# A Nyström attention and gated feed-forward kernel with the next pair's turns and sums, the Z product and the attention pieces placed elsewhere

## The chip, the cores and the metric

The kernel runs on one core of one Trainium2 chip. The metric is the device time of one execution in microseconds. Three runs of the kernel before took 339.7, 344.31 and 350.49 us (median 344.31). In the text PE is TensorE, DVE is VectorE, ACT is ScalarE, POOL is GpSimd, and SP is SyncE, which here only issues DMAs.

## The reference

Batch 8, 8 heads, 576 rows, head dimension 64. Queries and keys are averaged over groups of 18 rows to 32 landmarks; three softmaxes follow, a 32 by 32 matrix is inverted by six steps, and the product goes through a gated feed-forward.

```python
q_lm = q.reshape(B, H, m, S // m, D).mean(axis=3)          # m = 32
k_lm = k.reshape(B, H, m, S // m, D).mean(axis=3)
A  = sm(q, k_lm);  Bm = sm(q_lm, k_lm);  C = sm(q_lm, k)   # softmax of scale * a @ b.T
Z  = Bm.T / (norm1(Bm) * norminf(Bm) + 1e-6)               # per head
for _ in range(6):
    Z = 2 * Z - Z @ Bm @ Z
x = A @ Z @ C @ v                                          # heads side by side: 4608 x 512
out = ((x @ w1) * (x @ w2)) @ w3 @ w_out
```

## The kernel before, in words

The kernel folds the last two weight matrices into one, `w34 = w3 @ w_out`, and it never forms the attention output: C v and Z give a small matrix per head, which is multiplied into w1 and w2 ("G"), so that "U" computes both feed-forward inputs straight from the normalised A. All order is written by hand: the scheduler is off, and two strings of tokens, `PROLOGUE` and `PERIOD`, say in which order the pieces are issued to the five in-order engine queues. Batches go in pairs: while pair p is in its U and D work, the attention pieces of pair p+1 run between, and pair p+2 is loaded. There are four pairs and so four runs of `PERIOD`, called periods 0 to 3 here; the last has only U and D work.

The tokens, with two digits for batch of the pair and head half: F, one of 32 folding slots (two `prod` matmuls, and in every second slot a turn of a piece of w3); K, a load of q or k with cast (POOL queue); T, its transposing DMA (SP queue); L, its sums to landmarks on POOL (on DVE in `Y`, for pair 0); X, the exchange of the two half sums and the landmark matrices `lmk` and `qbd`; C, scores of the landmarks against k with exp on ACT and partial sums `es` on POOL; V, their product with v (`W` loads v); A, scores of q; B, SM, R, I0 to I5, the landmark matrix and its inversion; S, denominators of A; N, normalised A (`ahat`); Z, the small matrix `zt`; G, `gproj`; U, `up_unit` (8 matmuls, a cast on ACT, a product `ab` on DVE); D, `down_chunk` (8 matmuls, a copy on ACT, two stores); w, a load of w1 or w2 (POOL queue); E, the copy of a head's w1 and w2 to the other 64 partitions. A mark ' means the pair after. PSUM has 8 banks: `big` takes two and `small` one. In the prologue there is one `big` buffer, in the periods three.

Of the kernel before, what the change touches and what calls it, by code (L numbers as in the profile page):

```python
# [46 lines left out]
def kernel(  # L47
# [101 lines left out]
    def sums(b, t, eng):  # L149
        lp = pz.tile([128, H, 32], FP32, name="lp", bufs=4)  # L150
        tt = sts[b][t + "T"]
        if eng is nc.vector:
            nc.vector.tensor_reduce(out=lp, in_=tt.rearrange("p h j (l g) -> p h l j g", g=3),
                                    axis=AX.XY, op=ALU.add)
        else:
            s = pz.tile([128, H, P], FP32, name="ls", bufs=1)
# [1 line left out]
            eng.tensor_tensor(out=s, in0=s, in1=tt[:, :, 2, :], op=ALU.add)
            s3 = s.rearrange("p h (l g) -> p h l g", g=3)
            eng.tensor_tensor(out=lp, in0=s3[:, :, :, 0], in1=s3[:, :, :, 1], op=ALU.add)  # L160
            eng.tensor_tensor(out=lp, in0=lp, in1=s3[:, :, :, 2], op=ALU.add)
# [74 lines left out]
    def istep(p, it):  # L236
# [15 lines left out]
        else:  # L252
# [3 lines left out]
            tbd = pz.tile([128, 4, 4, 32], FP32, name="tbd", bufs=1)  # L256
            for x in range(2):
                nc.vector.tensor_tensor(
                    out=tbd[:, 2 * x:2 * x + 2],
                    in0=t6[:, 2 * x:2 * x + 2].unsqueeze(2).to_broadcast([128, 2, 4, 32]),  # L260
# [367 lines left out]
```

## Time and profile before

| | before |
|---|---|
| three runs | 339.7, 344.31, 350.49 us |
| profiled execution | 342.35 us, of which span 340.6 us |
| PE busy | 286.8 us, 84% |
| PE weight load | 164.0 us, 48% |
| DVE busy | 171.8 us, 50% |
| ACT busy | 123.8 us, 36% |
| POOL busy | 116.5 us, 34% |
| DMA | 46.68 MB, mean 137 GB/s |

Busy shares are averages over stages with different limits. The chain that ended last runs mostly through PE (19% of the span, more than all the other engines together), and the PE row of the 40 slices has its only 0 in the slice from 42.6 to 51.1 us.

### The profile page before, as it was taken

The numbers are of one execution on the slowest core, as the hardware profiler recorded it, in microseconds if no ns is written. First come the engines' busy times: TensorE is split into PE (matmuls) and PEld (weight loads), VectorE is DVE, ScalarE is ACT, GpSimd is POOL, SyncE is SP. The second block draws the span as 40 slices with busy tenths as digits, with TensorE's granted clock in tenths as the row PEclk, the third lists the DMA queues.
The fourth block names the chain that finished last, engine by engine and source line by source line (L and its number), as shares of the span: only waits on it lengthen the run. The fifth ranks groups of instructions, "written<-read, shape, count | busy, mean of one in ns | idle before, by whom it ended". The sixth has DMA issues, their size and how long they took to land. (4 is left out here: it accounts for less than half of the span.)

```text
span 340.6 us, 8360 instructions
## 1 busy us (share of the span) xinstructions
PE 286.8 (84%) x3584; PEld 164.0 (48%) x3584; DVE 171.8 (50%) x313; ACT 123.8 (36%) x209; POOL 116.5 (34%) x138
## 2 busy tenths in 40 slices
PE   3795705999978986687999998598999899999994
PEld 2243304655533355554545665353566664456651
DVE  6026340533895232658665357957426676624320
ACT  2013101421222344232565643245564435534532
POOL 2001401500399626309597430848762000000000
PEclk9998765999979998989999999879999999999998
DMA  8999998399999400497999289899932021132234
GB/s 203 295 258 175 174 219 188 53 210 185 176 226 213 89 2 2 65 172 122 194 213 230 64 125 167 126 183 203 231 81 49 28 60 36 31 93 64 69 84 126
DMA packets 66437, 46.68 MB, mean 137 GB/s; under 512 B 39264, under 2 KB 57696, under 8 KB 66400
## 3 DMA queue, kind: packets, MB, share of 16 engines
q1 hardware_dynamic: 49408, 28.32, 41.5%
q0 software_dynamic: 13600, 11.54, 23.6%
q10 hardware_dynamic: 3392, 6.29, 5.8%
q8 instruction: 28, 0.46, 0.6%
q14 instruction: 9, 0.07, 0.1%
HBM read 38.80 MB, written 9.44 MB: 142 GB/s over the span
## 5 line engine op out<-in xcount | busy, mean ns | idle before, releaser
L402 DVE TENSOR_TENSOR ab<-a_sb,big 128x576 f16<-128x576 f16 x64 | 48.2, 752 | 68.0 <-ACT a_sb L401 60.4
L395 PE MATMUL big<-ahat,gt 128*128 128x288 f16 x512 | 78.0, 296 | 4.1 <-DVE gt L380 1.9
L473 PE MATMUL psw<-wof,w3t 128*128 128x512 f32 x128 | 67.7, 659 | 1.8 <-DMA wof<-in_moe_w_out_dram 1.8
L423 PE MATMUL small<-w,ab 128*128 128x512 f16 x288 | 67.5, 380 | 0.3
L395 PEld LDWEIGHTS <-gt 128*128 128x128 f16 x512 | 48.2, 101 | 28.6 <-issue 11.1
L401 ACT CAST a_sb<-big 128x576 f16<-128x576 f32 x64 | 40.7, 636 | 25.1 <-PE big L395 22.7
L423 PEld LDWEIGHTS <-ab 128*128 128x128 f16 x288 | 26.8, 98 | 30.7 <-issue 2.5
L425 ACT ACTIVATE o_sb<-small 128x512 f32<-128x512 f32 x36 | 21.5, 597 | 53.1 <-PE small L423 53.1
L473 PEld LDWEIGHTS psw<-wof,w3t 128*128 128x128 f32 x128 | 23.9, 206 | 26.7 <-issue 23.2
L281 POOL TENSOR_TENSOR e<-ect 96x384 f32<-96x384 f32 x16 | 16.0, 998 | 52.3 <-ACT ect L276 49.8
L86 POOL DMA_DIRECT2D nat<-in_k_dram x8 | 6.4, 799 | 69.7 <-DMA kT<-nat 69.5
L292 PE MATMUL small<-vt,ect 96*32 96x64 f32 x768 | 15.0, 229 | 14.1 <-DMA vt<-in_v_dram 13.8
L380 DVE TENSOR_SCALAR gt<-big 128x1024 f16<-128x1024 f32 x16 | 19.2, 1216 | 8.6 <-PE big L373 8.6
L292 PEld LDWEIGHTS small<-vt,ect 96*32 96x32 f32 x768 | 12.2, 115 | 18.5 <-DMA vt<-in_v_dram 14.7
L373 PE MATMUL big<-wdup,zt 128*32 128x512 f16 x256 | 19.6, 384 | 1.4 <-DVE gt L380 0.9
L466 DVE COPY w3t<-pst 128x512 f32<-128x512 f32 x8 | 5.5, 692 | 28.5 <-PE pst L461 28.4
L378 ACT ACTIVATE gt<-big 128x1024 f16<-128x1024 f32 x16 | 16.4, 1023 | 7.5 <-PE big L373 7.4
L244 PE MATMUL small<-sz 32*32 32x64 f32 (+1 forms) x768 | 15.2, 217 | 4.3 <-DVE sz L250 2.7
L271 PE MATMUL big<-qbd,kT 128*96 128x64 f16 x192 | 12.6, 222 | 6.5 <-POOL qbd L176 3.0
L476 ACT CAST w<-psw 128x512 f16<-128x512 f32 x8 | 4.7, 585 | 34.7 <-PE psw L473 24.1
L276 ACT ACTIVATE ect<-big 96x768 f32<-96x768 f32 x16 | 12.8, 806 | 10.3 <-PE big L271 10.3
L244 PEld LDWEIGHTS small<-sz 32*32 32x32 f32 x768 | 11.5, 107 | 10.4 <-DVE sz L250 3.3
(85 smaller groups left out, 316.0 us busy)
## 6 DMA issues: line engine op xcount, KB each, us to landing
vt<-in_v_dram SPq DMA_DIRECT2D x8, 1152.0 KB, 12.3
nat<-in_k_dram POOLq DMA_DIRECT2D x8, 576.0 KB, 6.4
nat<-in_q_dram POOLq DMA_DIRECT2D x8, 576.0 KB, 9.2
out_dram<-o_sb SPq DMA_DIRECT2D x24, 192.0 KB, 2.3
w3f<-in_moe_w_dram ACTq DMA_DIRECT2D x16, 256.0 KB, 6.6
out_dram<-o_sb SPq DMA_DIRECT2D x24, 128.0 KB, 2.4
wof<-in_moe_w_out_dram ACTq DMA_DIRECT2D x4, 512.0 KB, 9.9
wdup<-in_moe_w_dram POOLq DMA_DIRECT2D x2, 1024.0 KB, 15.0
```

Source lines behind the costliest of these rows:

```text
L244: nc.tensor.matmul(psI[sl, 64 * a:64 * a + n], src[sl, a, 32:64], src[sl, a, 0:n], start=True, stop=True, tile_position=(32 * h, 32 * h))
L281: nc.gpsimd.tensor_tensor(out=e3, in0=ect[:, 0:3], in1=ect[:, 3:6], op=ALU.add)
L292: nc.tensor.matmul(psV[32 * h:32 * h + 32, 0:64], st["ect", qd][:, c, h, :], st["v"][:, 4 * qd + h, c, :], start=(c == 0), stop=(c == TK - 1),
L373: nc.tensor.matmul(psG[32 * h:32 * h + 32, n, :], st["zt"][:, 4 * qd + h, :], wdup[:, 4 * qd + h, w, 512 * n:512 * n + 512], start=True, s ...
L378: nc.scalar.activation(out=dst, in_=psG, func=AXF.Copy, scale=1.0 / ZS)
L380: nc.vector.tensor_scalar(out=dst, in0=psG, scalar1=1.0 / ZS, scalar2=None, op0=ALU.mult)
L395: nc.tensor.matmul(p[:, c, 0:HS], st["g", qd][:, w, 128 * j:128 * j + 128], st["ahat", qd][:, c, :], start=(qd == 0), stop=(qd == 1))
L401: nc.scalar.copy(out=a_sb, in_=p[:, :, 0:HS])
L402: nc.vector.tensor_tensor(out=ring["ab"][:, j, off:off + S].rearrange("p (c s) -> p c s", c=2), in0=a_sb, in1=pp[1][:, :, 0:HS], op=ALU.mult)
L423: nc.tensor.matmul(pso[:, :], w, w34[:, j, :], start=(j == 0), stop=(j == 7))
L425: nc.scalar.activation(out=o_sb, in_=pso[:, :], func=AXF.Copy, scale=1.0 / (X64 * X64))
L473: nc.tensor.matmul(psw[j], w3ts[j, c // 4][:, c % 4, :], wof[:, c, :], start=(c == 0), stop=(c == 7))
```

## The change

The strings are rewritten. The prologue has no N for batch 1 of pair 0 and two of its G pieces no more; these follow in the first period, marked +, which means "of the pair whose U work runs". A third string, `FIRST`, is used for period 0, and `PERIOD` for the others; the mark " loads three pairs ahead. Turns and sums (T and L) of the pair after the next begin in the first half of a period. `zmat` is done once for a pair, by 16 matmuls on 32 by 32 tiles of `t6`, where two masked block-diagonal products were; the mask and `tbd` are gone. The denominators stay in PSUM for reciprocal, cast and mix. The sums on POOL are cut in two halves of four heads each. The copies of the folding turns and of the exchange run on ACT.

```diff
+PROLOGUE = """
+F F F F F F F F F Y0 F F F Y1 F C00 F C01 w0 F A00 F A01 w1 F F B F SM C10 'Kk0 'Kq0 F R V00 F V01 I0 'Tk0 F C11 I1 'Kk1 F A10 I2 'Tq0 F V10 I3 'Lk0 'Kq1 E0 E1 F V11 A11 I4 F S0 I5 'Tk1 'Lq0 E2
+F E3 E4 E5 F N00 Z E6 E7 F N01 'Tq1 'W0 'W1 F G000 S1 'Lk1 F G001 F G010 'Lq1 F G011
+"""
+FIRST = """
+U +G100 'Kk0 'Kq0 U +G110 X0 U +G101 +N10 C00 U +N11 +G111 C01 X1 U A00 V00 'Tk0 U A01 V01 B 'Kk1 U SM C10 'Tq0 U A10 C11 'Kq1
+U R 'Lk0 D I0 V10 U I1 A11 'Lq0 D I2 V11 'Tk1 U I3 'Tq1 D I4 S0 U I5 'Lk1 D N00 S1 'W0 U Z N01 'W1 'Lq1 U G000 'X0 "Kk0 U G001 "Kq0 U G010 G011
+"""
 PERIOD = """
-U C00 D C01 U X1 A00 D V00 U A01 C10 D V01 B U C11 SM D V10 'Kk0 U R A10 D I0 V11 'Kq0 U I1 'Tk0 U S0 I2 'Tq0 'Kk1 U A11 I3
-U N00 'Lk0 I4 'Tk1 'Kq1 D N01 S1 U I5 'Lq0 'Tq1 D Z0 'W0 'W1 U N10 Z1 U N11 G000 D 'Lk1 G010 U 'X0 G001 U G011 D G100 'Lq1 U G110 U G101 G111
+U +G100 C00 D +G110 C01 U X1 +G101 'Tk0 A00 D V00 A01 'Kk1 +N10 U +G111 'Tq0 D B 'Kq1 V01 'Lk0 U SM C10 D A10 C11 'Lq0 U R D +N11 I0 U I1 A11 'Tk1 U V10 I2 U V11 I3 'Tq1 'Lk1
+U I4 D I5 S0 'X0 U Z 'Lq1 'W0 D N00 S1 'W1 U N01 G000 "Kk0 D G001 "Kq0 U G010 D G011 U U U U
 """
...
-PROLOGUE = """
-F F F F F F F Y0 F F C00 C01 F A00 Y1 F w0 V00 C10 F V01 C11 B F SM 'Kk0 A01 F 'Kq0 V10 R F I0 A10 'Tk0 F I1 S0 w1 F I2 V11 'Tq0 'Kk1 F N00 I3 'Tk1 'Kq1 F N01 I4 A11 'Lk0 F I5 'Tq1
-S1 F 'Lq0 E0 Z0 E1 F E2 E3 N10 Z1 F E4 E5 N11 F E6 E7 G000 'Lk1 F G010 'W0 F 'X0 G001 'W1 F G011 'Lq1 F G100 F G110 F G101 F G111 F
-"""
...
-            s = pz.tile([128, H, P], FP32, name="ls", bufs=1)
-            eng.tensor_tensor(out=s, in0=tt[:, :, 0, :], in1=tt[:, :, 1, :], op=ALU.add)
...
+            for h0 in range(0, H, 4):
+                hs = slice(h0, h0 + 4)
+                s = pz.tile([128, 4, P], FP32, name="ls", bufs=1)
+                eng.tensor_tensor(out=s, in0=tt[:, hs, 0, :], in1=tt[:, hs, 1, :], op=ALU.add)
...
-            nc.vector.tensor_copy(out=lx[t][0:64], in_=st["lp" + t][64:128])
+            (nc.scalar.copy if eng is nc.gpsimd else nc.vector.tensor_copy)(
+                out=lx[t][0:64], in_=st["lp" + t][64:128])
...
-        ect = pat.tile([P, TK, 4, 32], FP32, name="ect", bufs=2)
+        ect = pat.tile([P, TK, 4, 32], FP32, name="ect", bufs=3)
...
-        rr = pz.tile([128, QS], FP32, name="rr", bufs=1)
-        nc.vector.reciprocal(out=rr, in_=psS[:, 0:QS])
+        rr = psS[:, 0:QS]
+        nc.vector.reciprocal(out=rr, in_=rr)
...
+    def zmat(p):
+        t6 = prs[p]["t6"]
+        psZ = big()
+        for a in range(4):
+            xd = sts[2 * p + a // 2]["xd", a % 2]
+            for h in range(4):
+                sl = slice(32 * h, 32 * h + 32)
+                e = 64 * (h % 2)
+                nc.tensor.matmul(psZ[e:e + 64, h // 2, 32 * a:32 * a + 32], xd[sl, :], t6[sl, a, :],
+                                 start=True, stop=True, tile_position=(32 * h, e))
+        zt = pat.tile([128, 4, 2, 2, 32], FP16, name="zt", bufs=2)
+        for e in range(2):
+            pv_ = psZ[64 * e:64 * e + 64, :, 0:128].rearrange("p c (a m) -> p a c m", m=32)
+            nc.scalar.copy(out=zt[0:64, :, :, e, :], in_=pv_)
+            nc.vector.tensor_tensor(out=zt[64:128, :, :, e, :], in0=pv_, in1=zt[0:64, :, :, e, :],
+                                    op=ALU.subtract)
...
-        if cc == 0:
-            nc.vector.tensor_copy(out=dst, in_=pst)
-        else:
-            nc.scalar.copy(out=dst, in_=pst)
+        nc.scalar.copy(out=dst, in_=pst)
...
-        for tok in PERIOD.split():
+        for tok in (PERIOD if p else FIRST).split():
...
+            elif tok[0] == '"':
+                attn(p + 3, tok[1:])
+            elif tok[0] == "+":
+                attn(p, tok[1:])
```

Three places show what the tables move, all on POOL.

The first is POOL's queue in the middle of the prologue, before, from the fourth head half of C on (`e` and `es` are its partial sums, `nat` the loads of q and k of pair 1, `wdup` the load of w1 or w2, `ls` and `lp` the sums):

```order
L281 TENSOR_TENSOR e3_448<-ect_446 96x384
L283 TENSOR_TENSOR es_450<-e3_448 96x128
L284 TENSOR_TENSOR es_450<-es_450,e3_448 96x128
L86 DMA nat_495<-in_k_dram 96x8x384
L86 DMA nat_519<-in_q_dram 96x8x384
L489 DMA wdup_93<-in_moe_w2_dram 64x8x1024
L86 DMA nat_707<-in_k_dram 96x8x384
L86 DMA nat_747<-in_q_dram 96x8x384
L157 TENSOR_TENSOR ls_788<-kT_603 128x768
```

and of the change, from the second head half of C on:

```order
L283 TENSOR_TENSOR es_340<-es_340,e3_338 96x128
L486 DMA wdup_92<-in_moe_w1_dram 64x8x1024
L486 DMA wdup_92<-in_moe_w2_dram 64x8x1024
L280 TENSOR_TENSOR e3_451<-ect_449 96x384
L282 TENSOR_TENSOR es_453<-e3_451 96x128
L283 TENSOR_TENSOR es_453<-es_453,e3_451 96x128
L90 DMA nat_456<-in_k_dram 96x8x384
L90 DMA nat_458<-in_q_dram 96x8x384
L280 TENSOR_TENSOR e3_605<-ect_603 96x384
L282 TENSOR_TENSOR es_607<-e3_605 96x128
L283 TENSOR_TENSOR es_607<-es_607,e3_605 96x128
L90 DMA nat_628<-in_k_dram 96x8x384
```

Before, w1 goes out after the second half (not shown) and w2 behind the first two loads of pair 1; now both stand together, ahead of the first loads of pair 1.

The second is POOL's queue where pair 1's landmark matrices are made, before, at the end of the prologue (`lmk` and `qbd0` are X0):

```order
L160 TENSOR_TENSOR lp_921<-ls_922 128x256
L161 TENSOR_TENSOR lp_921<-lp_921,ls_922 128x256
L172 TENSOR_TENSOR lmk_958<-lp_787,lx_952 128x256
L176 TENSOR_TENSOR qbd0_89<-lp_847,lx_955 64x8x32 x2
L157 TENSOR_TENSOR ls_987<-qT_827 128x768
L158 TENSOR_TENSOR ls_987<-ls_987,qT_827 128x768
L160 TENSOR_TENSOR lp_986<-ls_987 128x256
L161 TENSOR_TENSOR lp_986<-lp_986,ls_987 128x256
L281 TENSOR_TENSOR e3_1091<-ect_1089 96x384
```

and of the change, in the first units of period 0:

```order
L161 TENSOR_TENSOR ls_992<-ls_992,qT_916 128x384
L163 TENSOR_TENSOR lp_986<-ls_992 128x128
L165 TENSOR_TENSOR lp_986<-lp_986,ls_992 128x128
L90 DMA nat_1040<-in_k_dram 96x8x384
L90 DMA nat_1042<-in_q_dram 96x8x384
L177 TENSOR_TENSOR lmk_1074<-lp_724,lx_1068 128x256
L181 TENSOR_TENSOR qbd0_88<-lp_848,lx_1071 64x8x32 x2
L280 TENSOR_TENSOR e3_1123<-ect_1121 96x384
```

X0 stood ahead of the last sum of pair 1; it now stands behind all four sums of that pair and behind two loads of pair 2.

The third is POOL's queue in period 1, before, between X1 and the third head half of C:

```order
L172 TENSOR_TENSOR lmk_2051<-lp_1806,lx_2045 128x256
L176 TENSOR_TENSOR qbd1_90<-lp_1903,lx_2048 64x8x32 x2
L281 TENSOR_TENSOR e3_2151<-ect_2149 96x384
L283 TENSOR_TENSOR es_2153<-e3_2151 96x128
L284 TENSOR_TENSOR es_2153<-es_2153,e3_2151 96x128
```

and of the change:

```order
L181 TENSOR_TENSOR qbd1_89<-lp_1852,lx_2062 64x8x32 x2
L90 DMA nat_2149<-in_k_dram 96x8x384
L90 DMA nat_2215<-in_q_dram 96x8x384
L160 TENSOR_TENSOR ls_2251<-kT_2079 128x384
L161 TENSOR_TENSOR ls_2251<-ls_2251,kT_2079 128x384
L163 TENSOR_TENSOR lp_2250<-ls_2251 128x128
L165 TENSOR_TENSOR lp_2250<-lp_2250,ls_2251 128x128
L160 TENSOR_TENSOR ls_2256<-kT_2079 128x384
L161 TENSOR_TENSOR ls_2256<-ls_2256,kT_2079 128x384
L163 TENSOR_TENSOR lp_2250<-ls_2256 128x128
L165 TENSOR_TENSOR lp_2250<-lp_2250,ls_2256 128x128
L280 TENSOR_TENSOR e3_2309<-ect_2307 96x384
```

Two loads and the whole first sum of pair 3 now stand ahead of the partial sums that V10 of pair 2 needs.

## Rows read from the trace of the kernel before

**Rows 1.** Windows by stage: start:end, length, busy per engine, PEclk, DMA share, GB/s.
```profile
0.00:122.90 122.90, 93.70 (x840) 47.44 (x841) 55.01 (x108) 24.45 (x42) 38.89 (x47) 0.90 0.97 184
122.90:179.50 56.60, 46.41 (x809) 29.66 (x809) 33.93 (x60) 25.31 (x43) 32.54 (x37) 0.94 0.73 119
179.50:240.90 61.40, 54.67 (x849) 32.53 (x849) 38.46 (x70) 28.66 (x48) 33.75 (x38) 0.94 0.88 159
240.90:295.20 54.30, 51.74 (x849) 31.06 (x850) 30.29 (x60) 27.82 (x46) 11.29 (x18) 1.00 0.28 70
295.20:327.20 32.00, 31.47 (x200) 19.51 (x200) 13.21 (x17) 14.24 (x25) 0.00 (x0) 1.00 0.27 69
327.20:340.60 13.40, 8.83 (x42) 3.83 (x40) 0.94 (x2) 3.37 (x6) 0.00 (x0) 0.92 0.43 112
```

**Rows 2.** Timeline of PE in the prologue: start, us, operation [idle before <- releaser].
```profile
19.14 3.60 PE L473 MATMUL psw<-wof,w3t 128*128 128x512 f32 x8
23.01 3.60 PE L473 MATMUL psw<-wof,w3t 128*128 128x512 f32 x8
...
34.25 3.76 PE L473 MATMUL psw<-wof,w3t 128*128 128x512 f32 x4
...
54.52 1.51 PE L292 MATMUL small<-vt,ect 96*32 96x64 f32 x48 [13.84 <-DMA vt<-in_v_dram]
```

**Rows 3.** Timeline of the waits in periods 0 and 1.
```profile
131.91 0.68 PE L271 MATMUL big<-qbd,kT 128*96 128x64 f16 x12 [2.70 <-POOL qbd L176]
...
214.60 1.65 POOL L157 TENSOR_TENSOR ls<-kT 128x768 f32<-128x768 f16 x1
...
214.75 1.60 DVE L333 CAST rhi<-rr 128x144 f16<-128x144 f32 x1
...
219.95 1.19 PE L355 MATMUL small<-tbd,xd 128*128 128x128 f32 x4 [3.30 <-DVE tbd L258]
```

**Rows 4.** Timeline of several engines, 37 to 51 us.
```profile
37.49 0.70 POOL L489 DMA_DIRECT2D wdup<-in_moe_w_dram  x1
...
47.37 2.55 DVE L153 TENSOR_REDUCE lp<-qT 128x256 f32<-128x2304 f16 x1 [4.53 <-DMA qT<-nat]
...
50.01 0.40 ACT L170 COPY lx<-lp 64x256 f32<-64x256 f32 x1 [6.67 <-DVE lp L153]
```

**Rows 5.** Landing times, by tile: weight halves, loads of q and k, turns of k.
```profile
DMA to landing us min/median/max: 13.5/15.0/16.4
...
DMA to landing us min/median/max: 5.0/7.1/18.1
...
DMA to landing us min/median/max: 5.8/8.4/16.9
```

**Rows 6.** Timeline of POOL, the first and last row of pair 1's sums.
```profile
88.62 0.77 POOL L86 DMA_DIRECT2D nat<-in_k_dram  x1 [21.60 <-DMA kT<-nat]
...
115.99 0.80 POOL L161 TENSOR_TENSOR lp<-lp,ls 128x256 f32<-128x256 f32 x1
```

**Rows 7.** Groups by line and form, POOL: busy, mean ns of one, idle before.
```profile
L281 POOL TENSOR_TENSOR e<-ect 96x384 f32<-96x384 f32 x16 | 16.0, 998 | 52.3 <-ACT ect L276 49.8 <-PE small L187 1.8 <-PE big L395 0.5
...
L157 POOL TENSOR_TENSOR ls<-kT 128x768 f32<-128x768 f16 x6 | 9.9, 1643 | 8.5 <-DMA kT<-nat 8.4
```

**Rows 8.** Timeline of PE in periods 1 to 3, for the pitch of the pieces.
```profile
198.37 0.45 PE L230 MATMUL small<-btn,bt 32*32 32x32 f32 x32 [0.21 <-DVE btn L220]
...
279.99 0.66 PE L355 MATMUL small<-tbd,xd 128*128 128x128 f32 x4
...
281.59 0.41 PE L343 MATMUL big<-rmix,selc 128*128 128x144 f16 x4
281.93 0.62 PE L373 MATMUL big<-wdup,zt 128*32 128x512 f16 x8
...
316.17 1.89 PE L423 MATMUL small<-w,ab 128*128 128x512 f16 x8
317.90 2.12 PE L395 MATMUL big<-ahat,gt 128*128 128x288 f16 x16
```

More of the change, by code (lines that the diff above doesn't have):

```diff
@@ L116, in constants @@
                                 base=0, pattern=[[-1, 128]], channel_multiplier=1)
-        nc.vector.memset(ones1, 1.0)
+        nc.vector.memset(ones1, 1.0 / ZS)
         for t in qbds:
@@ L155, in sums @@
         else:
-            s = pz.tile([128, H, P], FP32, name="ls", bufs=1)
-            eng.tensor_tensor(out=s, in0=tt[:, :, 0, :], in1=tt[:, :, 1, :], op=ALU.add)
[L158 to L161, printed above, removed]
+            for h0 in range(0, H, 4):
+                hs = slice(h0, h0 + 4)
+                s = pz.tile([128, 4, P], FP32, name="ls", bufs=1)
+                eng.tensor_tensor(out=s, in0=tt[:, hs, 0, :], in1=tt[:, hs, 1, :], op=ALU.add)
+                eng.tensor_tensor(out=s, in0=s, in1=tt[:, hs, 2, :], op=ALU.add)
+                s3 = s.rearrange("p h (l g) -> p h l g", g=3)
+                eng.tensor_tensor(out=lp[:, hs], in0=s3[:, :, :, 0], in1=s3[:, :, :, 1],
+                                  op=ALU.add)
+                eng.tensor_tensor(out=lp[:, hs], in0=lp[:, hs], in1=s3[:, :, :, 2], op=ALU.add)
         sts[b]["lp" + t] = lp
@@ L255, in istep @@
                                     op=ALU.add)
[L256 to L260, printed above, removed]
-                    in1=mask4.unsqueeze(1).to_broadcast([128, 2, 4, 32]), op=ALU.mult)
-            prs[p]["tbd"] = tbd
+            prs[p]["t6"] = t6
     def cscores(b, qd):
@@ L300, in cv @@
         nc.vector.reciprocal(out=rcr, in_=psV[:, 64:65])
-        xd = pz.tile([128, 2, 64], FP32, name="xd", bufs=4)
-        nc.scalar.activation(out=xd, in_=psV[:, 0:64].unsqueeze(1).to_broadcast([128, 2, 64]),
-                             func=AXF.Copy, scale=rcr[:, 0:1])
+        xd = pz.tile([128, 64], FP32, name="xd", bufs=4)
+        nc.scalar.activation(out=xd, in_=psV[:, 0:64], func=AXF.Copy, scale=rcr[:, 0:1])
         st["xd", qd] = xd
@@ L347, in norm_a @@
         st["ahat", qd] = a
-    def zmat(b):
-        st = sts[b]
-        x = b % 2
-        tbd = prs[b // 2]["tbd"]
-        psZ = small()
-        for qd in range(2):
-            nc.tensor.matmul(psZ[:, 128 * qd:128 * qd + 128],
-                             st["xd", qd].rearrange("p a d -> p (a d)"),
-                             tbd[:, 2 * x + qd].rearrange("p h m -> p (h m)"),
-                             start=True, stop=True)
-        zt = pat.tile([128, 8, 32], FP16, name="zt")
-        pzv = psZ[:, 0:256].rearrange("p (h m) -> p h m", m=32)
-        nc.scalar.activation(out=zt, in_=pzv, func=AXF.Copy, scale=ZS)
-        nc.vector.scalar_tensor_tensor(out=zt[64:128], in0=pzv[64:128], scalar=ZS,
-                                       in1=zt[64:128], op0=ALU.mult, op1=ALU.subtract)
-        st["zt"] = zt
+    def zmat(p):
[14 more added lines that the diff above has]
+                                    op=ALU.subtract)
+        for x in range(2):
+            sts[2 * p + x]["zt"] = zt[:, 2 * x:2 * x + 2].rearrange("p a c e m -> p (a c e) m")
     def gproj(b, qd, w):
@@ L503, in attn @@
             return bnorm(p)
+        if tok == "Z":
+            return zmat(p)
         if kind in "BR":
@@ L516, in attn @@
             return exchange(b, nc.gpsimd)
-        if kind == "Z":
-            return zmat(b)
         if kind == "S":
```

5 lines of the change are left out of this document (1 added, 4 removed).

## The prediction

> **What bounds the kernel now.** I read the trace by stage first, because the busy shares of the page average over stages with different limits. The windows [rows 1] give the prologue 122.9 us, periods 0 to 3 56.6, 61.4, 54.3 and 32.0 us, and the tail 13.4 us. PE is the longest engine in each. In period 3 it is full: 31.5 of 32.0 us. Period 2 is the yardstick of a whole period: 9 D, 16 U and all attention pieces in 54.3 us at granted clock 1.00, with POOL at 11.3 us, since no sums are left there. Period 1 holds the same pieces and needs 7 us more, and period 0, which runs 5 D fewer (D has a pitch of 1.73 us [rows 8]), needs 2.3 us more where it should need 8.7 us less. So some 11 us of period 0 and 7 us of period 1 are waits, and much more of the prologue: PE is busy in 93.7 of 122.9 us.
>
> The timeline says which waits. In the prologue PE stands for 13.8 us before the first V, until v has landed [rows 2], and the fold slot after an idle stretch takes 3.76 us where a warm pair of slots takes 3.60 us [rows 2]; that is the lower clock, worth about 2 us each time. In period 0, C waits 2.70 us for the landmark matrix that POOL makes, and in period 1, Z waits 3.30 us for the masked product on DVE; that product was late because a cast of DVE took 1.60 us, from 214.75 on, beside a 1.65 us sum of POOL that began at 214.60 [rows 3].
>
> **The change, part by part.** I add up the new time from five stretches, against the span of 340.6 us of the profiled execution.
>
> *The prologue up to the first C of period 0.* V is asked for only after 20 fold slots, so the wait for v goes. What is late next: ACT's exchange copies for the second batch wait for DVE's sum of q, which waited 4.53 us for its turn and began at 47.37 [rows 4]; ACT also carries the exps, so the second C of the new order, with one `big` buffer, stops PE until then. A weight load went out at 37.49 [rows 4] beside that turn, and in the new order it is not yet out. So the sum of q begins between 42.8 (no wait) and 47.4; I take 44, nearer the first. With 2.55 us for the sum and 0.40 us for the copy, PE goes on at about 48, having stood about 9 us after 14 fold slots.
>
> From there a chain on POOL and the DMAs decides. Two rounds of C, exp and partial sums (estimate 6 us, from 1.0 us for `e` alone [rows 7]) put both weight loads out at about 53. They stand together ahead of pair 1's loads on one queue. One lands after 13.5 to 16.4 us [rows 5]: both may be through after 16.4 us if they share nothing else (69), or after twice 16.4 (86); I take twice 13.5, so 80, because the 15 us of one were measured beside other traffic that is there still. The load of k follows at its shortest, 5.0 us, as it has waited in line, and its turn at its shortest, 5.8 us, as the weights that slowed it are through [rows 5]: 91. Then the old chain from the landing of that turn, 88.62, to the last sum, 116.8, took 28.2 us [rows 6]; four sums, one X and two loads lay in it. The new one has two loads more at 0.77 us each, and does not wait for the q turn between. A sum is now eight halves: half of 1643 ns is 0.82 us, and the 384-element row `e` costs 998 ns [rows 7], so a sum is between as long as before and 1 us longer. I take 27 us, with X0 last. The first C of period 0 runs at 118. PE alone would be there at about 106: from 48, 18 slots at 1.94 us (two take 3.87, from 19.14 to 23.01 [rows 2]) are 35 us, and two thirds of the other 31.6 us of PE work of the prologue (93.7 [rows 1] less 32 slots) are 21 us, of which 3.3 us of G and N moved behind; with them and three U it comes to 5.5 us for what stands ahead of that C. So PE waits there some 12 us.
>
> *The rest of period 0.* The yardstick 54.3 less 5 D (8.65) less the pieces ahead of C (3 U at 1.06, 3 G at 0.62, one N at 0.41 [rows 8]: 5.45) is 40.2 us. Z as 16 small matmuls is priced by R, which is 16 of them too, 32 records in 0.45 us, against two old ones at 0.66 us [rows 8]: 0.9 us less for a pair, 39.3. Added: about 1.4 us at B, since X1 stands behind two rounds of partial sums on POOL, 1 us at G, since no D covers `zt`, and 1.8 us for the low clock after the wait: 43.5.
>
> The Trainium skill, "TensorE: Matmul & The Clock Gate", section "Wait — 56ns, not 53.3ns?", puts a floor of about 25 ns under each matmul, however small. By it the 32 records of Z would take 0.8 us and the four pairs 1.4 us more than by the row, whose 32 records take 14 ns each; the sum below would be 1.4 us longer, and the row decides.
>
> *Period 1.* 54.3 less 0.9, and the DVE waits of the old one are gone, as cast, mix and Z read PSUM and `tbd` is no more. But the sum of pair 3 now stands on POOL ahead of the partial sums that V10 waits for, and it waits for a load and a turn first. Nothing shows that wait; it is between 0 (nine microseconds of PE work lie between) and a whole sum of 5.4 us; I take 2: 55.4.
>
> *Period 2* has no sums, in old and new: 53.4. *Period 3* gets 4 G and 2 N: 32.0 + 2.5 + 0.8 = 35.3. *The tail* has the same five D: 13.4.
>
> Edits at nothing: the folding copies on ACT (36% busy), the exchange copies on ACT (four in a row, behind which a U may wait a microsecond, in the 2 us above), the third buffer of `ect`, and the mask. If ACT were full they would cost some 0.4 us each.
>
> Sum: 118 + 43.5 + 55.4 + 53.4 + 35.3 + 13.4 = 319. The profiled execution took 342.35 us with a span of 340.6, so 1.75 us lie around it: 320.7. It stands 0.6% under the median of the runs, which spread by 3%; I add nothing for it. **320.5 us.**
>
> **The rivals.**
> 1. *The turns come early and PE is the bound.* If the weight loads land side by side, C runs at about 107 and PE does not wait: 11 us less and no low clock, 306 of span, 308 us. For it: one half alone landed after 13.5 us with v in flight [rows 5]. Against it: the loads share a queue.
> 2. *The chain is late, but less than the gain.* Weights at 86, k at its median 7.1, the turn at 8.4 [rows 5]: 101.5, C at 128.5, 331 us. The same time comes from V10 waiting a whole sum in period 1 with waits as long in period 0.
> 3. *The periods are not denser.* The new places meet new waits as long as the old: period 0 keeps 56.6 less 5.45, period 1 61.4, period 2 54.3. With the rest as above, 333.4 of span and 335 us, just over 2% under the median. A mechanism: the normalisation SM has two-input operations in SBUF, and C's partial sums and the new sums run near it on POOL. For it: the 1.60 us cast [rows 3]. Against it: in the new order most late DVE operations read PSUM, and POOL's pieces are half as long.
> 4. *Slower.* Loads and turns at the slowest that the trace shows, one after the other: weights out at 56, 32.8 us for both, k 18.1, turn 16.9 [rows 5], 27 us of POOL: C at 151, 353 us. Each microsecond there is one of time, as nothing else can be moved ahead of X0; from C at about 139 on the kernel is slower than the profiled run, and from 146 by 2%. Against it: the 18.1 and 16.9 belong to the stretch in which load, turn and weights overlapped, and that no longer happens.
>
> The page on SBUF of the Trainium skill, "SBUF — State Buffer", section "Who interferes with whom", says that VectorE and GpSimd share a port pair as a lock, held by whoever starts first for a whole instruction, and that operations with two SBUF inputs take part. By that rule up to three operations of SM could each wait a half sum, 0.8 to 1.0 us, which would be rival 3; the 1.60 us cast agrees with the lock, and no row shows SM beside a sum.
>
> **How the numbers follow.** Forecast 0.45, rival 1 0.20, rival 2 0.16, rival 3 0.12, rival 4 0.07. The range is 305 to 335: it takes in rivals 1 and 2 and the near half of rival 3, and leaves out rival 4, the rest of rival 3 and a little below 305. Within 2% of 344.31 is 337.4 to 351.2, about what a measurement of this kernel can tell from no change. Faster by more: 0.86 (forecast, rivals 1 and 2, part of 3); within: 0.08; slower: 0.06.
>
> **What would show it.** Right: the wait for v is gone, and PE shows instead a wait of about 9 us from about 39 on, released by ACT's exp, and one of about 12 us before the first C of period 0, ended by POOL's `qbd`; the last sum of pair 1 ends near 115; Z takes under 0.6 us a pair, and its wait on DVE is gone; period 1 takes about 55 us and period 3 35 us. Wrong: C of period 0 after 130 (the chain was mis-sized), or period 1 at 60 us or more (the pieces only moved the waits). I should be most wrong where both weight loads meet on one queue, since no row shows two of them together.

## The result, and the profile after

The changed kernel takes **325.92 us** (median of four runs, 322.49 to 329.0) against 343.14 us for the kernel before in the same session: a ratio of 0.9458, 95% interval 0.9293 to 0.9624. It is faster. A ratio takes only the runs of each kernel that lie within 1.5% of its fastest, which is why it differs from the ratio of the two medians, and the profiled execution of the changed kernel, 1.52% above its fastest run, lies just outside. The forecast was 320.5 us, the range 305 to 335 us. The profiled execution took 327.4 us with a span of 325.5 us, 0.5% above the median.

The stage windows of the changed kernel, cut at the first U of each period as in [rows 1] (start:end, length, then busy time of PE, PEld, DVE, ACT and POOL, granted clock, DMA share, GB/s):

```profile
0.00:107.47 107.47, 86.45 (x824) 44.51 (x825) 40.58 (x87) 25.93 (x46) 39.07 (x58) 0.94 1.05 203
107.47:164.03 56.56, 46.78 (x833) 27.86 (x832) 28.80 (x54) 28.60 (x51) 41.32 (x61) 0.95 0.91 161
164.03:224.10 60.07, 54.89 (x878) 32.18 (x875) 31.18 (x62) 29.86 (x53) 34.97 (x52) 0.94 0.88 159
224.10:277.30 53.20, 51.25 (x874) 30.44 (x872) 29.80 (x56) 28.31 (x49) 9.85 (x15) 1.00 0.18 46
277.30:312.20 34.90, 34.75 (x241) 20.29 (x240) 15.69 (x20) 16.76 (x28) 0.00 (x0) 1.00 0.26 69
312.20:325.50 13.30, 8.80 (x42) 3.82 (x39) 0.91 (x2) 3.33 (x6) 0.00 (x0) 0.99 0.38 100
```

Against [rows 1] the prologue loses 15.4 us, period 0 keeps its 56.6 us, period 1 loses 1.3 and period 2 1.1, period 3 gains 2.9 (the G and N that came to it). Read alone, this says that the prologue's order did it. That reading is wrong, as the experiments show: the same prologue order in the kernel before wins nothing, and without it the change still wins 11.0 of its 17.2 us.

PE's timeline of the changed kernel's prologue (start, duration, operation, [idle before <- releaser]); it answers to [rows 2]:

```profile
47.38 1.10 PE L270 MATMUL big<-qbd,kT 128*96 128x64 f16 x12 [8.44 <-ACT ect L275]
...
64.18 0.88 PE L291 MATMUL small<-vt,ect 96*32 96x64 f32 x48
...
92.58 0.75 PE L355 MATMUL big<-t,xd 32*64 32x32 f32 x32 [3.04 <-DVE ahat L344]
93.25 3.55 PE L470 MATMUL psw<-wof,w3t 128*128 128x512 f32 x4
...
99.42 1.98 PE L470 MATMUL psw<-wof,w3t 128*128 128x512 f32 x4
...
105.53 0.62 PE L373 MATMUL big<-wdup,zt 128*32 128x512 f16 x8 [1.13 <-ACT gt L378]
107.47 1.14 PE L395 MATMUL big<-ahat,gt 128*128 128x288 f16 x8 [1.33 <-DVE gt L380]
...
114.38 0.41 PE L341 MATMUL big<-rmix,selc 128*128 128x144 f16 x4 [1.58 <-ACT a_sb L401]
115.26 0.70 PE L270 MATMUL big<-qbd,kT 128*96 128x64 f16 x12 [0.47 <-DVE ab L402]
```

The first V stands at 64.18 without a wait, where it had waited 13.84 us. In its place come 8.44 us ahead of the second C, 3.04 us ahead of Z (its `big` buffer was held until DVE had made `ahat`, behind four `wdup` copies of 4.76 us together), a slow fold slot behind that (3.55 against 1.98 us), and waits of 1.1 to 1.6 us between G, the first U and N, where no fold slot is left to lie between them.

POOL's chain for the next pair, and ACT's copies that end it, in the changed kernel (the same columns; they answer to [rows 6]):

```profile
64.84 0.80 POOL L90 DMA_DIRECT2D nat<-in_k_dram  x1
...
80.88 0.79 POOL L90 DMA_DIRECT2D nat<-in_k_dram  x1 [6.21 <-DMA kT<-nat]
...
107.98 0.49 POOL L165 TENSOR_TENSOR lp<-lp,ls 128x128 f32<-128x128 f32 x1
...
112.89 0.72 POOL L177 TENSOR_TENSOR lmk<-lp,lx 128x256 f16<-128x256 f32 x1 [2.92 <-ACT lx L175]
113.58 1.51 POOL L181 TENSOR_TENSOR qbd<-lp,lx 64x256 f16<-64x256 f32 x2
```

```profile
110.95 1.02 ACT L378 ACTIVATE gt<-big 128x1024 f16<-128x1024 f32 x1 [0.18 <-PE big L373]
112.00 0.40 ACT L173 COPY lx<-lp 64x256 f32<-64x256 f32 x1
...
113.27 0.40 ACT L175 COPY lx<-lp 64x256 f32<-64x256 f32 x1
113.69 0.64 ACT L401 CAST a_sb<-big 128x576 f16<-128x576 f32 x1
```

POOL's last sum ends at 108.5, but the exchange copies run at 112.0, because ACT has two `a_sb` and two `gt` to make first. POOL waits 2.92 us for ACT. And the four copies in a row (1.67 us) hold up the next `a_sb`, for which N waits 1.58 us. X0 on POOL then ends at 115.1 and C runs at 115.3. So the first C is set by the order of PE and ACT, with X0 at its end, and not by the time at which POOL's sums are done.

The one long wait of period 1, PE in the changed kernel:

```profile
191.79 0.88 PE L291 MATMUL small<-vt,ect 96*32 96x64 f32 x48
195.91 0.29 PE L296 MATMUL small<-ones,es 96*32 96x1 f32 x8 [3.24 <-POOL es L283]
196.13 1.07 PE L249 MATMUL small<-sz 32*32 32x64 f32 x32
197.13 2.10 PE L395 MATMUL big<-ahat,gt 128*128 128x288 f16 x8
...
207.50 0.67 PE L355 MATMUL big<-t,xd 32*64 32x32 f32 x32
```

V10 stands 3.24 us for `es`, and the next steps run at the lower clock (I 1.07 against 0.65 us, U 2.10 against 1.15). Z takes 0.67 us for a pair and no longer waits for DVE, where it had waited 3.30 us [rows 3].

### The profile page after: what moved, and what is told of

The parts are those of the page before. It is cut to its first block, busy times and chain, and to the rows that moved or that the text cites. A ratio compares the mean times of both kernels' runs of the same rounds, so it can differ in the third digit from the quotient of the medians.

```text
span 325.5 us, 8594 instructions
## 1 busy us (share of the span) xinstructions
PE 282.9 (87%) x3680; PEld 159.1 (49%) x3680; DVE 146.9 (45%) x280; ACT 132.8 (41%) x229; POOL 125.2 (38%) x186
## 4 chain that ended last, share of the span: by engine, by line
PE 58%; DMA 15%; DVE 11%; ACT 8%; issue 3%; POOL 3%; SPq 0%; ACTq 0%; POOLq 0%; DVEq 0%
PE small L423 17%; PE big L395 13%; PE psw L470 10%; DMA nat<-in_k_dram 6%; DMA kT<-nat 6%; PE big L373 5%; PE small L291 3%; PE small L249 3%; DMA qT<-nat 3%; ACT a_sb L401 3%; DVE ab L402 2%; PE big L270 2%; DVE lp L154 2%; DVE wdup L490 1%; ACT o_sb L425 1%
## 5 line engine op out<-in xcount | busy, mean ns | idle before, releaser
L395 PE MATMUL big<-ahat,gt 128*128 128x288 f16 x512 | 76.5, 292 | 7.9 <-ACT a_sb L401 2.9
L470 PE MATMUL psw<-wof,w3t 128*128 128x512 f32 x128 | 65.7, 648 | 1.0 <-DMA wof<-in_moe_w_out_dram 1.0
L373 PE MATMUL big<-wdup,zt 128*32 128x512 f16 x256 | 20.8, 406 | 2.2 <-ACT gt L378 1.1
L270 PEld LDWEIGHTS <-kT 128*96 128x96 f16 x192 | 11.2, 133 | 13.3 <-issue 12.8
L154 DVE TENSOR_REDUCE lp<-kT 128x256 f32<-128x2304 f16 x2 | 5.1, 2552 | 27.7 <-DMA kT<-nat 27.7
L465 ACT COPY w3t<-pst 128x512 f32<-128x512 f32 x16 | 9.4, 584 | 18.5 <-PE pst L461 18.5
L249 PE MATMUL small<-sz 32*32 32x64 f32 (+1 forms) x768 | 15.9, 221 | 0.0
L461 PE MATMUL pst<-ident,w3f 128*128 128x128 f32 x64 | 10.6, 292 | 6.1 <-DMA w3f<-in_moe_w_dram 6.1
```

Source lines behind the costliest of these rows:

```text
L249: nc.tensor.matmul(psI[sl, 64 * a:64 * a + n], src[sl, a, 32:64], src[sl, a, 0:n], start=True, stop=True, tile_position=(32 * h, 32 * h))
L270: nc.tensor.matmul(flat[0:P, 64 * i:64 * i + 64], st["kT"][:, 4 * qd + h, j, :], st["qbd"][:, 4 * qd + h, :, :].rearrange("p a m -> p (a m)"),
L373: nc.tensor.matmul(psG[32 * h:32 * h + 32, n, :], st["zt"][:, 4 * qd + h, :], wdup[:, 4 * qd + h, w, 512 * n:512 * n + 512], start=True, s ...
L395: nc.tensor.matmul(p[:, c, 0:HS], st["g", qd][:, w, 128 * j:128 * j + 128], st["ahat", qd][:, c, :], start=(qd == 0), stop=(qd == 1))
L470: nc.tensor.matmul(psw[j], w3ts[j, c // 4][:, c % 4, :], wof[:, c, :], start=(c == 0), stop=(c == 7))
```

## The experiments

Each row is one kernel; the ratio is to the kernel before, run beside it. The stages are those of its profiled execution: to the first U, period 0, period 1, all that follows. The kernels ran in four sessions, the changed kernel in the first alone; the kernel before had a median of 343.1 us beside it, 343.4 beside the kernels 1 to 4, 343.7 beside 5 to 8 and 341.5 beside 9 to 12. The runs of one kernel spread by 3 to 12 us, and each has one profiled execution, so a difference of a few microseconds from the changed kernel is no more than likely.

| kernel | median us | ratio, 95% interval | to first U | p0 | p1 | rest |
|---|---|---|---|---|---|---|
| before | 343.1 | | 122.9 | 56.6 | 61.4 | 99.7 |
| changed | 325.9 | 0.946, 0.929 to 0.962 | 107.5 | 56.6 | 60.1 | 101.4 |
| 1 new code, old order | 343.6 | 0.985, 0.973 to 0.997 | 123.0 | 57.6 | 56.8 | 105.0 |
| 2 old prologue order | 332.5 | 0.967, 0.958 to 0.977 | 115.1 | 56.5 | 57.7 | 101.5 |
| 3 new prologue, old rest | 343.0 | 0.998, 0.994 to 1.003 | 121.6 | 59.1 | 58.8 | 99.6 |
| 4 first sum later | 330.5 | 0.967, 0.959 to 0.974 | 108.5 | 57.3 | 61.4 | 101.4 |
| 5 sum ahead of load | 327.9 | 0.953, 0.944 to 0.962 | 109.0 | 57.0 | 58.5 | 101.4 |
| 6 weight copies later | 325.5 | 0.946, 0.937 to 0.955 | 106.0 | 57.4 | 58.2 | 101.4 |
| 7 loads sooner | 327.2 | 0.951, 0.941 to 0.960 | 108.5 | 57.5 | 57.7 | 101.5 |
| 8 all three | 327.5 | 0.957, 0.945 to 0.969 | 107.6 | 56.5 | 58.0 | 101.5 |
| 9 old code, G in period 0 | 339.3 | 0.989, 0.980 to 0.997 | 111.8 | 68.3 | 59.3 | 99.7 |
| 10 three code edits undone | 328.5 | 0.960, 0.954 to 0.966 | 112.3 | 53.9 | 59.0 | 101.4 |
| 11 half of lx on DVE | 322.9 | 0.940, 0.932 to 0.948 | 108.8 | 53.5 | 58.8 | 101.4 |
| 12 best of all | 321.1 | 0.937, 0.932 to 0.943 | 106.3 | 54.1 | 57.3 | 101.3 |

The theory after the two traces: nearly all of the gain is the prologue's order. The rivals: the code edits carry it, or the order of the periods.

**1. New code, old order.** Both tables of the kernel before, Z as one token:

```diff
-PROLOGUE, FIRST, PERIOD of the changed kernel
+PROLOGUE, PERIOD of the kernel before (FIRST = PERIOD), Z0 -> Z, Z1 left out
```

> The changed kernel's code (Z in 32-row tiles, denominators in PSUM, halved POOL sums, first lx copies on ACT, third buffers) with the old order of the work everywhere: prologue and all four periods as in the kernel before. Theory (nearly all of the gain is the order of the prologue): the stretch up to the first C of period 0 stays near 122 us, the periods lose only the waits on the DVE cast, mix and tbd, 1 to 3 us together, so 338 to 343 us in all. Rival (the code edits carry the gain): 326 to 332 us, with the prologue near 110.

Measured 343.6 us, the same median as before (343.4); the interval of the ratio reaches from 0.973 to 0.997. The prologue stays at 123.0 us. Period 1 loses 4.6 us, as the waits on the cast, the mix and `tbd` are gone; in the profiled execution 5.3 us came back from period 2 on, so the total shows little of it. The code edits alone don't carry the gain.

**2. The old prologue order, all else as changed.**

```diff
-F F F F F F F F F Y0 F F F Y1 F C00 F C01 w0 F A00 F A01 w1 F F B F SM C10 ... V00 F V01 ...
+F F F F F F F Y0 F F C00 C01 F A00 Y1 F w0 V00 C10 F V01 C11 B F SM ...   (no N10 N11 G1xx 'X0)
```

> The changed kernel with the old order of the prologue alone (without the N10, N11, G1xx and X0 of it that now stand in period 0); the periods as changed. Theory: the prologue takes 119 to 121 us (the old 122.9 without 2.8 us of G and N), the periods as in the changed kernel, so 337 to 342 us. Rival (the order of the periods carries the gain, by a sooner turn and sum): 326 to 331 us.

Measured 332.5 us, between the two. The wait for v is there in full, and yet the first U starts 7.8 us sooner than before; the timeline of PE of this kernel:

```profile
54.45 1.51 PE L291 MATMUL small<-vt,ect 96*32 96x64 f32 x48 [15.18 <-DMA vt<-in_v_dram]
...
56.92 3.39 PE L470 MATMUL psw<-wof,w3t 128*128 128x512 f32 x4
```

The theory gave too little to the rest: 11.0 us under the kernel before, of the 17.2 us of the whole change, came without the prologue's order. In the profiled spans that is 7.8 us of prologue, as N10, N11, the four G1xx (four, where the section on the change says two) and X0 moved into a period 0 that did not grow (56.5 us), and 3.7 us of period 1, less 1.8 us behind it.

**3. The new prologue order in the kernel before.**

```diff
-PROLOGUE of the kernel before
+PROLOGUE of the changed kernel, Z -> Z0 Z1, C10 behind V00, and at its end:
+F G100 F G110 F 'X0 G101 N10 F N11 G111
```

> The kernel before with the new order of the prologue alone (C10 stands behind V00 since the old code has two ect buffers; N10, N11, the G1xx and X0 follow at its end), old code and old periods. Theory: the prologue falls from 122.9 to about 110 us (107.5 of the changed kernel and 2.8 us of G and N), the rest stays at 217.7 us, so 327 to 332 us. Rival (code edits or the period order carry it): 338 to 343 us.

Measured 343.0 us, ratio 0.998: nothing. The theory falls here. PE's timeline, from the end of the fold on:

```profile
104.22 2.11 PE L473 MATMUL psw<-wof,w3t 128*128 128x512 f32 x4
106.27 0.62 PE L373 MATMUL big<-wdup,zt 128*32 128x512 f16 x8
108.01 0.61 PE L373 MATMUL big<-wdup,zt 128*32 128x512 f16 x8 [1.13 <-ACT gt L378]
109.95 0.61 PE L373 MATMUL big<-wdup,zt 128*32 128x512 f16 x8 [1.33 <-DVE gt L380]
111.69 1.04 PE L373 MATMUL big<-wdup,zt 128*32 128x512 f16 x8 [1.12 <-ACT gt L378]
113.86 1.05 PE L373 MATMUL big<-wdup,zt 128*32 128x512 f16 x8 [1.12 <-ACT gt L378]
116.23 0.64 PE L343 MATMUL big<-rmix,selc 128*128 128x144 f16 x4 [1.32 <-DVE gt L380]
...
121.56 2.08 PE L395 MATMUL big<-ahat,gt 128*128 128x288 f16 x8 [1.33 <-DVE gt L380]
```

The fold ends at 106.3 instead of 122.3 us: v's wait is gone, as expected. But the fold slots are a fixed number, 32, and they were the cover under which the G, with one `big` buffer, waited for their copies. Spent on v, they are missing here: G, N and X0 stand alone for 15.3 us, of which PE is busy 6.2, at a granted clock of 0.67. The wait was moved, not removed.

**9. The same, with those pieces among the first U of period 0.** Old code, and old order otherwise; `FIRST` and `+` are handled as in the changed kernel.

```diff
-U C00 D C01 U X1 A00 D V00 U A01 C10 D V01 B U C11 SM D V10 ...
+U +G100 U +G110 X0 U +G101 +N10 C00 U +N11 +G111 C01 X1 A00 D V00 A01 C10 D V01 B C11 SM D V10 ...
```

> The kernel before with the new order of the prologue, as in the run of the new prologue with the old rest, but with the N10, N11, the four G1xx and X0 that stood uncovered behind its last fold slot (106.3 to 121.6 us there) put between the first four U of period 0. Old code, old periods otherwise (that period's pieces of the next pair follow in the old order). Theory (the gain needs both: v's wait taken out of the fold and the G beside the U): the first U starts at 108 to 111 us, period 0 takes 57 to 59, the rest as before, so 328 to 333 us. Rival (old code or old period order holds it back at another place, the POOL chain with whole sums first): 336 to 343 us.

Measured 339.3 us. The first U is at 111.8, 11.1 us sooner than before, and period 0 is 11.7 us longer, so that period 1 begins at 180.1, where it began at 179.5 in the kernel before. The window of period 0 in this kernel, then PE's longest waits in it (us in total, times, longest):

```profile
111.80:180.09 68.29, 55.57 (x849) 34.52 (x849) 39.18 (x66) 28.01 (x47) 35.63 (x41) 0.83 0.64 104
```

```profile
PE big L275 <- POOL qbd L180: 4.8, 2, 3.9
PE small L359 <- DVE tbd L262: 3.9, 1, 3.9
...
```

PE is busy 9 us longer than in the old period 0, some 2.8 of it with the pieces that came; over the rest the granted clock fell from 0.94 to 0.83. So the rival was right: the old code and the old order of period 0 hold it back. Of the 17.2 us, 11.0 come without the prologue's order (kernel 2), and the rest needs both halves: with the new code and periods the same prologue order is worth 6.5 us (kernel 2 against the changed one; the intervals of their ratios touch), with the old ones 0.4 and 2.2 (kernels 3 and 9, by the medians). What takes up the pieces in period 0 is its new order, Z without `tbd` or the third buffers of `ect` and `es`; these weren't separated, but kernel 10 below, whose period 0 is as short without them, excludes the halved sums, half of the exchange copies on ACT and the denominators in PSUM. And no kernel has the new order of the periods with the old code, so how much of the 11.0 us is the order alone isn't shown; the new code in the old order wins nothing by the medians and 0.3% to 2.7% by the interval of its ratio (kernel 1).

**4. The first sum of the pair two ahead behind C11** in the periods 1 to 3.

```diff
-... V01 'Lk0 U SM C10 D A10 C11 'Lq0 ...
+... V01 U SM C10 D A10 C11 'Lk0 'Lq0 ...
```

> The changed kernel with the first sum of the pair two ahead ('Lk0) moved behind C11 in the periods 1 to 3, so that POOL makes the es of C10 and C11 before it. Theory: in period 1 the wait of V10 on es (3.24 us) and the slow clock behind it go, period 1 falls from 60.1 to about 55 us and the time by 3 to 5 us. Rival (the POOL chain is what counts, and a later sum moves the wait to X0, the first C and the G of the next period): period 1 or the start of period 2 gets the time back, no change within 1 us.

Measured 330.5 us, no gain. V10's wait is gone, and in period 1 PE stands at another place, a few instructions on, 4.36 us "issue": it waits for nothing that the profile shows, in the middle of one step I.

```profile
196.95 0.41 PE L249 MATMUL small<-sz 32*32 32x64 f32 x13
201.72 0.84 PE L249 MATMUL small<-sz 32*32 32x64 f32 x19 [4.36 <-issue]
```

Neither theory had named it; the last section shows what stands behind it.

**5. The first sum ahead of the load of q.** PE's order stays.

```diff
-... 'Tq0 D B 'Kq1 V01 'Lk0 U SM ...
+... 'Tq0 D B V01 'Lk0 'Kq1 U SM ...
```

> The changed kernel with, in the periods, the first sum of the pair two ahead ('Lk0) ahead of the load of q ('Kq1) on POOL instead of behind it; PE's order is the same. In the changed kernel POOL stood 8.4 us at that load (until the turn of q landed), made the sum then, and V10 waited 3.24 us for its es. Theory: the sum runs in those 8.4 us, es is there in time, period 1 falls from 60.1 to 55 to 57 us and the time by 3 to 5 us. Rival (the pause without a named releaser of 4.4 us, met in the run with the sum behind C11, is what V10's wait hid, as PE's instructions at that place are not there sooner): period 1 stays at 59 to 63 us, no gain.

Measured 327.9 us against the changed kernel's 325.9, so no gain. `es` is there in time, and a pause of 1.51 us stands at the same matmul (the first of the 19) instead. Period 1 falls from 60.1 to 58.5 us, between the theory (55 to 57) and the rival (59 to 63). The gain of 1.6 us in that stage is smaller than the spread of the runs.

**6. The `wdup` copies later in the prologue.**

```diff
-... E2 F E3 E4 E5 F N00 Z E6 E7 F N01 'Tq1 'W0 'W1 F G000 S1 ...
+... E2 F F N00 Z E3 F N01 E4 E5 'Tq1 'W0 'W1 F G000 S1 E6 E7 ...
```

> The changed kernel with the copies of wdup that DVE makes ahead of N00 in the prologue (four, 4.76 us) put behind N00, Z, N01 and S1. Theory: Z's wait on ahat (3.04 us) and the slow fold slot behind it (3.55 against 1.98 us) go, the first U starts at 103 to 104 us instead of 107.5, C of period 0 follows since POOL's last sum ended at 108.5 and lx only waited for ACT, so 3 to 4.5 us less in all. Rival (the POOL chain sets C): C stays at 115, what is won in the prologue is lost as a wait on qbd, within 1 us of the changed kernel.

Measured 325.5 us, no difference. Z's wait falls to 0.85 us and the fold ends 3.3 us sooner (100.6), but with fewer fold slots left behind it PE waits twice between G (1.27 and 1.12 us, not once), and the first U is only 1.5 us sooner; that U runs at the lower clock (2.08 against 1.14 us), N waits 1.75 us for `a_sb`, and C stands at 115.5, where it was at 115.3. POOL is not what holds it: over the kernels 5 to 8 its last sum ends at 107.9 to 109.5, and X0 then waits 3.2 to 6.5 us for ACT's copies. V10's wait is gone here too, without an edit to it, and the pause of 1.53 us stands in its place.

**7. The loads of the next pair ahead of the second weight load.**

```diff
-... A01 w1 F F B F SM C10 'Kk0 'Kq0 F R V00 F V01 I0 'Tk0 F C11 I1 'Kk1 F A10 I2 'Tq0 ...
+... A01 'Kk0 'Kq0 w1 F F B F SM C10 'Tk0 F R V00 F V01 I0 'Tq0 F C11 I1 'Kk1 F A10 I2 ...
```

> The changed kernel with the loads of k and q of the next pair's first batch ahead of the second weight load and of C10's sums on POOL, and their turns two to three tokens sooner; PE, DVE and ACT keep their order. Theory (PE's own order sets C, POOL's chain ended 3.5 us ahead of the lx copies): the chain's last sum ends at 98 to 104 us instead of 108.5, C of period 0 moves by less than 1 us and the time stays within 1 us. Rival (the chain sets C, as the prediction had it): C and the time fall by what the chain gains, 5 to 9 us.

Measured 327.2 us. The load of k went out 13.1 us sooner (51.78 instead of 64.84), but beside the weights, which now landed after 11.1 to 21.9 us (9.8 to 14.6 in the changed kernel); the loads of k and q took 13.7 and 17.3 us and the turn of k 14.0, and that turn had landed at 80.2, where it was 80.9. That the DMA engines' time is short in this stretch, and not the place in the queue, fits their share of 1.09 up to the first U (1.05 in the changed kernel); no run takes traffic away to show it. The last sum ended at 109.2, so this run doesn't tell what a shorter chain would do. It does show POOL waiting 4.57 us for ACT's copies at X0.

**8. The three edits 5 to 7 together.**

> The changed kernel with the three edits together: the sum ahead of the load in the periods, the wdup copies later, the loads sooner. Theory: the gains add, 3 to 5 of period 1 and 3 to 5 of the prologue, with the chain out of the way: 6 to 10 us under the changed kernel. Rival: one of them only moves its wait, 0 to 4 us.

Measured 327.5 us: no gain, nearer to the rival. The small gains don't add; the pauses and slow stretches come back elsewhere.

**10. Three code edits undone under the new order.**

```diff
-            for h0 in range(0, H, 4):   # halves
+            s = pz.tile([128, H, P], FP32, name="ls", bufs=1)   # whole
...
-            (nc.scalar.copy if eng is nc.gpsimd else nc.vector.tensor_copy)(out=lx[t][0:64], ...
+            nc.vector.tensor_copy(out=lx[t][0:64], ...
...
-        rr = psS[:, 0:QS]
+        rr = pz.tile([128, QS], FP32, name="rr", bufs=1)
```

> The changed kernel with three of its code edits undone: POOL's sums whole instead of in halves, the first of the lx copies back on DVE, the denominators' reciprocal in SBUF instead of PSUM. The order is as changed. Theory (order carries the gain): within 3 us of the changed kernel, the DVE cast of rhi long again (1.6 us) where a sum runs beside it, the a_sb waits behind lx shorter by 0.8 us each. Rival (the edits matter under the new order): 4 to 10 us slower than the changed kernel.

Measured 328.5 us, within 3 us of the changed kernel, so these three edits together don't carry the gain. Inside, two effects of opposite sign show: the prologue is 4.8 us longer, and period 0 is 2.7 us shorter. In the prologue a mix takes 2.44 us beside POOL's whole sums, and Z waits 5.24 us for `ahat`:

```profile
88.55 2.44 DVE L329 SCALAR_TENSOR_TENSOR rmix<-rhi,lomask,rr 128x144 f16<-128x144 f16 x1
...
96.75 1.08 PE L351 MATMUL big<-t,xd 32*64 32x32 f32 x32 [5.24 <-DVE ahat L340]
```

The eight casts of `rhi` take 0.23 to 1.65 us, as long as the theory had it at the worst, and the eight mixes 0.37 to 2.44 us, where those of the changed kernel take 0.31 and 0.36 us, all of them. The two effects can be told apart: kernel 11 below ran in the same session and differs from this one by the halved sums and the denominators in PSUM alone. Its ratio is 0.940 (0.932 to 0.948) against 0.960 (0.954 to 0.966) here, by the medians 5.6 us. So these two edits do matter under the new order, and undone together with the copies on ACT, which cost period 0 some 2.4 to 3.0 us, most of their worth does not show.

**11. Half of the exchange copies back on DVE.**

```diff
-            (nc.scalar.copy if eng is nc.gpsimd else nc.vector.tensor_copy)(
-                out=lx[t][0:64], in_=st["lp" + t][64:128])
+            nc.vector.tensor_copy(out=lx[t][0:64], in_=st["lp" + t][64:128])
```

> The changed kernel with the first lx copy of each pair of copies on DVE again. Theory: ACT's four copies (1.67 us) become two (0.8), so N10's wait of 1.58 us and U's of 1.74 us behind a_sb fall by 0.8 each, 1 to 2.5 us in all. Rival: DVE's copies wait on POOL's sums there or take longer beside them, and the ab products behind them come later: no gain within 1 us.

Measured 322.9 us, 3.0 us under the changed kernel's median, where the theory had 1 to 2.5; the runs reach from 319.7 to 329.2 and the intervals of the two ratios overlap, so that the kernel is faster than the changed one is not shown by the time. What the edit does to period 0 is shown: it falls from 56.6 to 53.5 us, and to 53.9 and 54.1 in kernels 10 and 12, which have the same edit; no kernel of the new order without it (2, 4 to 8) is under 56.4. The window of period 0 in this kernel:

```profile
108.75:162.30 53.55, 47.11 (x833) 28.04 (x833) 30.84 (x60) 25.69 (x45) 39.33 (x58) 0.94 0.90 157
```

N's wait falls from 1.58 to 0.62 us, and what ends C's wait is now POOL's `qbd` (0.90 us). At the end of the period the same four copies stand ahead of another `a_sb`; PE waits there 1.74 us in the changed kernel (the first line), and not at all in this one (the second):

```profile
160.41 1.85 PE L395 MATMUL big<-ahat,gt 128*128 128x288 f16 x8 [1.74 <-ACT a_sb L401]
...
159.72 1.44 PE L394 MATMUL big<-ahat,gt 128*128 128x288 f16 x8
```

**12. Edits 5, 6 and 11 together.**

> The changed kernel with the wdup copies later, the sum ahead of the load and the first lx copy on DVE. Theory: the small waits fall together, 2 to 5 us under the changed kernel: 321 to 324 us. Rival: the pause of PE in period 1 and the slow clock at the first U take them back, within 1 us of it.

Measured 321.1 us (320.64 to 325.89), the lowest of all, just inside the theory's 321 to 324. Its ratio to the kernel before, 0.937 (0.932 to 0.943), overlaps that of the changed kernel, 0.946 (0.929 to 0.962), so that it beats the kernel before is shown, and that it beats the changed one is likely but not shown.

## Why the prediction was right, and where it was not

The forecast of 320.5 us was 5.4 us (1.7%) low; the measured time lies inside the range, and it is faster as forecast. The span of 325.5 us is 6.5 us over the sum of 319: the six terms missed by -2.7, +5.3, +4.7, -0.2, -0.4 and -0.1 us. Step by step:

- **The wait for v goes: right**, and so are the places of what came instead in the first half: 8.44 us ahead of the second C, released by ACT's exp, ending at 47.4 (predicted 9 us, to 48), and the weight loads out at 51.8 (53).
- **POOL's chain sets the first C of period 0, at 118: the time was near (115.3), the reason failed.** The two weight loads landed after 9.8 to 14.6 us, not one after the other at 80; the turn of k had landed by 80.9 instead of 91. From there to the end of X0 27 us were predicted and 34.2 passed: the last sum ended at 108.5 and not near 115, but 27.6 us after the turn where the forecast left 24, and X0 then waited for ACT's copies and ended at 115.1. PE, forecast to be there at 106, came at 114.4: it lost 3.04 us at Z, 1.6 us to the slow fold slot behind it and 4.0 us at G, the first U and N. These 8.7 us were in no term. PE's predicted wait of 12 us for `qbd` was not there. That the time of the first C came out near is luck: the turn was ten microseconds sooner, and PE and X0 were later by nearly as much.
- **The rest of period 0: 43.5 predicted, 48.8 measured.** The term that failed is the exchange copies on ACT, put at nothing beside "a U may wait a microsecond". ACT is 41% busy over the changed kernel's span, but four copies in a row stand ahead of an `a_sb`, and a U waits 1.74 us for it and then runs at the lower clock (1.85 against 1.15 us). Moving half of the copies back to DVE shortens period 0 by 2.4 to 3.0 us (kernels 12, 10 and 11), a part of it ahead of the first C. From that C on the stretch takes 46.3, 46.6 and 44.7 us in kernels 11, 10 and 12, and 46.1 to 48.4 in the kernels 2 and 4 to 8, which keep the four copies; so the copies are worth some 2 to 3 of the 5.3 us, no more exactly than the others spread. The others are spread over waits of 0.2 to 1.0 us on `ect`, `btn`, `rmix`, `ab` and `zt` and a pause of 0.78 us, and weren't separated.
- **Period 1: 55.4 predicted, 60.1 measured**, the "60 us or more" that was to show it wrong. The mechanism was named and its size was not: V10 waited 3.24 us instead of 2, and the lower clock behind it, not priced, slowed two I, two U and V11 by 2.7 us together. Where that wait is gone (kernels 2, 5, 6, 8 and 12) the period takes 57.3 to 58.5 us, as PE then pauses 1.5 to 2.4 us in all a little further on, and 61.4 us in kernel 4, where the pause is 4.36 us. Kernel 7, where V10 still waits 2.13 us, takes 57.7. So taking the wait away gained little, and the pause was in no term either.
- **Period 2, period 3 and the tail: 53.4, 35.3 and 13.4 predicted; 53.2, 34.9 and 13.3 measured.** Where POOL has no sums, the sum of row by row holds within 0.4 us.
- **Z: 0.67 us a pair** (0.75 in the prologue), over the 0.6 that was to show the price right; its wait on DVE's `tbd` is gone. The row of R gave 0.45; the Trainium skill, "TensorE: Matmul & The Clock Gate", section "Wait — 56ns, not 53.3ns?", has a floor of about 25 ns per matmul, by which an estimate is 0.8 us. The trace does not agree: the 32 records of Z take 21 ns each, under the page's floor and over the row of R, and many of them start 6 or 7 ns after the one ahead.
- **Rival 3** (the periods are not denser) was half right: it had 51.2 us for the rest of period 0 (48.8 measured) and 61.4 for period 1 (60.1), though not by the named mechanism. R waits 0.71 us for SM's last result, no more. (Its terms add up to 333.6 us, not 333.4.)

That a shorter prologue by itself is worth what it loses in length was tacitly assumed. Kernels 3 and 9 show that it wasn't in this kernel: the time came back within 15 us in the one and within one period in the other.

## What to carry to other kernels

A filler with a fixed number of slots can hide one wait or another, not both: before you spend it on the longest wait, count what it covered there, and give that work another cover in the same change. An engine that is 41% busy still sets the time where several of its copies stand in a row ahead of the one result that the bound engine waits for; price the row, not the share. Undo edits one at a time: three undone together came out near nothing (kernel 10), though they held two that win and one that costs. And when a wait is taken away, look at what it hid: here PE came sooner to a place a few instructions on, paused there, and most of the expected gain stayed out.
